# Attention with a soft mixture of experts: another order of steps in the pair loop, another pacing of the weight loads, another tail

## The chip, the cores and the metric

The kernel runs on one core of a Trainium2 chip. The metric is device time in microseconds (us) of one execution. A profiled run also has a span, from its first to its last instruction, some 2 us under that time. A run that is over 1.5% above the fastest of the same kernel counts as slow, and only fast runs are compared.

In the lines of the profile PE is TensorE's matmuls, PEld its weight loads, DVE is VectorE, ACT ScalarE and POOL GpSimd; SBUF and PSUM are the memories on the chip. "Clock" is the share of TensorE's full clock that was granted. The DMA share is the mean busy share of the core's 16 DMA engines; 1.06 is what the fullest long stretches show. In brackets stands how long the engine was idle before, and what ended that; "issue" means that it waited for nothing that the profile shows.

## The reference

Eight batches of eight heads, 576 positions of 64 numbers; 16 "beacon" keys and values stand ahead of each head's own. The result of the attention, as x of shape (4608, 512), goes through a soft mixture of eight experts.

```python
# attention, for each of 64 heads
scores = scale * q @ concat(beacon_k, k).T        # 576 x 592, causal on the last 576
a = exp(scores - max); a /= a.sum(-1)
x = a @ concat(beacon_v, v)
# soft mixture of experts, over all 4608 tokens
logits = x @ phi                                  # 4608 x 32
d = softmax(logits, axis=0)                       # over tokens
slot_input = d.T @ x                              # 32 slots x 512, four for each expert
slot_out[e] = relu(slot_input[e] @ w1[e]) @ w2[e] # w1: 512 x 1024, w2: 1024 x 512
out = softmax(logits, axis=1) @ slot_out
```

The column softmax runs over all tokens, so the experts can't begin before the last head is done, and no output before the last expert.

## The kernel before

Two heads make a pair; 32 pairs run one after the other. For a pair, TensorE turns q and k (`Tq`, `Tk`), makes scores in four steps (`s0` to `s3`) that alternate between two PSUM buffers, ScalarE takes exponentials, GpSimd masks the diagonal blocks, TensorE multiplies with v for the pair before (`a0`, `a1`), and VectorE normalizes. x is turned (`xt`) for the logits (`lg`); once a batch the slot inputs are summed (`dt`, `si`).

The experts' weights are 33.5 MB in HBM. They come in 32 pieces, cast to 16 bits on the way, on GpSimd's DMA queue. q and k come on SyncE's queue, five pairs ahead.

```python
def load_w(i):                       # one piece: 1 MB read, 512 KB written
    ...
    nc.gpsimd.dma_start(out=arena[:, wloc[m]:wloc[m] + WP], in_=src)

wl = 0
for n in range(NP):                  # 32 pairs
    if n < 6:
        head(n)
    else:
        for op in ("s0", "s1", "V", "Tq", "a0", "lg", "s2", "Tk", "s3", "dt", "si", "a1", "xt"):
            step(op, n, b, g)
    ...                              # v loads of later batches, also on GpSimd's queue
    want = n if n < 6 else n - (n - 1) // 4 if n < 24 else 18 + 9 * (n - 23) // 5
    while wl < min(want, NPC):       # pieces asked for by the end of pair n
        load_w(wl)
        wl += 1
while wl < NPC:
    load_w(wl)
    wl += 1
```

After the loop: the last pair's attention, its x turned, logits, slot inputs, then the experts, first layer two steps ahead of the second, and the output.

```python
for p in range(EP + 2):              # EP = 4 steps of two experts
    if p < EP:
        first_layer(p)
    if p == 1:
        col_sums(0, 1)
        slot_factors()
    if 0 < p <= EP:
        turn_hidden(p - 1)
    if p > 1:
        second_layer(p - 2)
```

The softmax here doesn't subtract the row's maximum and nothing guards it: scores larger than these inputs give would overflow.

## Time and profile before

| | before |
|---|---|
| time, median of 4 runs | 197.15 us (195.99 to 200.28) |
| span of the profiled run | 194.7 us |
| first exponential of pair 6, of pair 31 | 37.5 us, 144.7 us |
| last weight piece landed | 163.05 us |
| first output issued | 168.0 us |

Read the table as a chain: loop, tail with experts, output. The output itself, 9.4 MB, takes the 26.7 us from 168.0 to the end. The lines of the profile behind it are in the prediction below.

### The profile page before, as it was taken

What the parts mean: (1) busy time and instruction counts of PE and PEld (TensorE: products, weight loads), DVE (VectorE), ACT (ScalarE), POOL (GpSimd) and SP (SyncE); (2) the same over time, 40 slices, a digit from 0 to 9 for tenths busy, and PEclk for the clock granted to TensorE, in tenths of its full rate; (3) what the DMA queues carried; (4) which work ended last, traced back from release to release, by engine and by line L of the source; (5) the groups of instructions that cost most, each with busy time, mean ns of one, the idle gap of its engine ahead of it and who ended that gap; (6) DMA issues with size and microseconds to landing.
All of it is one profiled execution on the core that took longest, in us unless ns stands there. A gap on an engine that the chain in (4) does not pass through costs nothing. (4 is left out here: it accounts for less than half of the span.)

```text
span 194.7 us, 7324 instructions
## 1 busy us (share of the span) xinstructions
PE 156.7 (81%) x3123; PEld 106.8 (55%) x3123; DVE 138.6 (71%) x286; ACT 128.3 (66%) x175; POOL 112.5 (58%) x293
## 2 busy tenths in 40 slices
PE   6778986779999888968999799988878699887400
PEld 2445765646776665646767566656656544454100
DVE  5537697578989888985799699788657342799700
ACT  2697763748997778775889678877795222578500
POOL 8659893945897597778778687666756100000000
PEclk9955899979999999996999999999999889999955
DMA  6999999999999999999999999999999990399994
GB/s 183 264 240 350 271 242 266 280 261 265 311 261 265 260 276 258 278 255 304 272 282 260 255 293 261 256 254 222 211 213 215 213 186 19 105 380 417 416 428 199
DMA packets 20464, 50.84 MB, mean 261 GB/s; under 512 B 5456, under 2 KB 5456, under 8 KB 19408
## 3 DMA queue, kind: packets, MB, share of 16 engines
q0 software_dynamic: 8048, 21.74, 56.3%
q1 hardware_dynamic: 12240, 28.35, 40.6%
q8 instruction: 24, 0.39, 0.8%
q10 hardware_dynamic: 144, 0.29, 0.5%
q14 instruction: 8, 0.07, 0.1%
HBM read 62.65 MB, written 9.44 MB: 370 GB/s over the span
## 5 line engine op out<-in xcount | busy, mean ns | idle before, releaser
L294 ACT ACTIVATE ex<-sc 128x736 f16<-128x736 f32 (+1 forms) x124 | 101.5, 870 | 27.4 <-PE sc L287 25.4
L296 POOL TENSOR_SCALAR_AFFINE_SELECT ex<-ex 128x256 f16<-128x256 f16 (+1 forms) x155 | 57.3, 399 | 31.4 <-ACT ex L294 31.0
L287 PE MATMUL sc<-qT,kT 64*128 64x336 bf16 (+5 forms) x384 | 44.9, 302 | 4.4 <-ACT ex L294 2.1
L309 PEld LDWEIGHTS <-ex 128*128 128x128 f16 (+1 forms) x930 | 37.5, 108 | 16.9 <-issue 14.8
L309 PE MATMUL av<-vh,ex 128*128 128x65 f16 x840 | 39.6, 200 | 6.3 <-issue 3.4
L270 PE MATMUL tr<-idb,arena 64*64 64x64 bf16 x1152 | 32.0, 201 | 6.6 <-DMA arena<-in_k_dram 2.3
L270 PEld LDWEIGHTS <-arena 64*64 64x64 bf16 x1152 | 25.4, 114 | 20.2 <-issue 13.3
L276 DVE COPY kT<-tr 128x576 bf16<-128x576 bf16 x27 | 20.4, 756 | 9.6 <-PE tr L270 9.6
L320 DVE TENSOR_TENSOR xb<-av,r 128x640 f16<-128x640 f32 x31 | 25.6, 825 | 1.1
L276 DVE COPY qT<-tr 128x576 bf16<-128x576 bf16 x32 | 23.2, 725 | 4.0 <-PE tr L270 3.9
L287 PEld LDWEIGHTS <-kT 64*128 64x128 bf16 (+1 forms) x384 | 15.9, 102 | 14.1 <-issue 6.1
L151 DVE STREAM_TRANSPOSE vh<-vbuf 128x256 f32<-128x256 f32 x32 | 20.4, 657 | 3.3 <-DMA vbuf<-in_beacon_v_dram 1.9
L183 POOL DMA_DIRECT2D arena<-in_moe_w_dram x32 | 17.9, 560 | 0.2
L698 ACT ACTIVATE arena<-fp,rc 128x512 f32<-128x512 f32 (+1 forms) x18 | 11.3, 677 | 7.4 <-PE fp L696 5.9
L127 POOL DMA_DIRECT2D vbuf<-in_v_dram x27 | 15.1, 571 | 0.2 <-DVE xb L320 0.2
L340 DVE COPY xT<-tr 128x592 f16<-128x592 f16 x31 | 13.9, 455 | 1.0 <-PE tr L332 1.0
L332 PE MATMUL tr<-idh,xb 128*128 128x128 f16 (+1 forms) x160 | 14.2, 221 | 0.1
L700 DVE TENSOR_SCALAR arena<-fp,rc 128x512 f32<-128x512 f32 (+1 forms) x19 | 13.1, 732 | 1.2 <-PE fp L696 0.4
L696 PE MATMUL fp<-soh,eLh 128*128 128x512 f16 (+1 forms) x37 | 10.6, 373 | 2.5 <-ACT arena L698 1.7
L319 DVE RECIPROCAL r<-av 128x10 f32<-128x10 f32 x31 | 6.8, 218 | 7.9 <-PE av L309 7.5
L332 PEld LDWEIGHTS <-xb 128*128 128x128 f16 (+1 forms) x160 | 10.4, 103 | 1.1 <-issue 0.9
L696 PEld LDWEIGHTS <-eLh 128*128 128x128 f16 x37 | 3.9, 114 | 5.7 <-issue 4.5
(101 smaller groups left out, 135.6 us busy)
## 6 DMA issues: line engine op xcount, KB each, us to landing
arena<-in_moe_w_dram POOLq DMA_DIRECT2D x32, 512.0 KB, 10.0
arena<-in_q_dram SPq DMA_DIRECT2D x32, 288.0 KB, 14.6
arena<-in_k_dram SPq DMA_DIRECT2D x31, 288.0 KB, 14.9
out_dram<-arena SPq DMA_DIRECT2D x8, 1024.0 KB, 7.2
vbuf<-in_v_dram POOLq DMA_DIRECT2D x30, 128.0 KB, 8.4
arena<-in_v_dram POOLq DMA_DIRECT2D x4, 128.0 KB, 8.4
out_dram<-arena SPq DMA_DIRECT2D x2, 256.0 KB, 3.5
out_dram<-arena SPq DMA_DIRECT2D x1, 512.0 KB, 4.0
```

Of the source, the lines that this page charges most:

```text
L127: nc.gpsimd.dma_start(out=vbuf[b % 2][32 * qd:32 * qd + 32, :], in_=bass.AP(tensor=v.tensor, offset=v.offset + lo, ap=[hs_, cs_, [1, TK * ...
L151: nc.vector.transpose(out=dst[:, e], in_=src.bitcast(FP).rearrange("p (j e) -> p e j", j=TK)[:, e])
L183: nc.gpsimd.dma_start(out=arena[:, wloc[m]:wloc[m] + WP], in_=src)
L270: nc.tensor.transpose(tp[po:po + 64, j, :], hi, idb[po:po + 64, po:po + 64])
L276: nc.vector.tensor_copy(out=dst, in_=src)
L287: nc.tensor.matmul(sc[0:kn, a, col:col + un], kT[n % 3][64 * a:64 * a + 64, P * c:P * c + kn], qT[n % 3][64 * a:64 * a + 64, u0:u0 + un], ...
L294: nc.scalar.activation(e, sc[:, :, 0:w], AF.Exp, scale=scale)
L296: nc.gpsimd.affine_select(out=e[0:m, :, o:o + m], in_=e[0:m, :, o:o + m], compare_op=AL.is_ge, fill=0.0, base=0, pattern=[[0, 2], [1, m]], ...
L309: nc.tensor.matmul(dst[0:m, i * DD:(i + 1) * DD], ex[n][0:kn, o + a * w:o + a * w + m], vchunk(b, 2 * g + a, c, kn), start=(c == 0), stop= ...
L320: nc.vector.tensor_tensor(out=xb[b % 2][:, :, 2 * g:2 * g + 2, :].rearrange("p i a d -> p a i d"), in0=avv[:, :, :, 0:D], in1=r5[:, :, :]. ...
L332: nc.tensor.transpose(tp[:, i, 0:m], xb[b % 2][0:m, i, 2 * g:2 * g + 2, :].rearrange("p h d -> p (h d)"), idh[0:m, 0:m])
L696: nc.tensor.matmul(fp_[:, c], etok(cg, j), soh[:, c], start=True, stop=True)
```

## The change

Its intent: ask for fewer weights while the loop runs, so that q, k and v get the DMA engines, and load the rest behind the loop; place q's turn and x^T so that ScalarE waits less for scores; and take work out of the way between the loop and the experts, with three filler matmuls to keep TensorE's clock up. `warm_tail(3)` makes the three fillers, matmuls whose results nobody uses. At the end of pair 31, 22 instead of 32 pieces are asked for.

```diff
-            for op in ("s0", "s1", "V", "Tq", "a0", "lg", "s2", "Tk", "s3", "dt", "si", "a1", "xt"):
+            for op in ("s0", "Tq", "s1", "V", "a0", "xt", "s2", "Tk", "s3", "lg", "a1", "dt", "si"):
                 step(op, n, b, g)
...
-        want = n if n < 6 else n - (n - 1) // 4 if n < 24 else 18 + 9 * (n - 23) // 5
+        want = n // 2 if n < 24 else 12 + 5 * (n - 23) // 4
...
     for rows in ((4,), (3, 2, 1), (0,)):
-        if rows == (0,):
-            spread_rows(0, nc.vector)
         for a in range(2):
             attend_blocks(...)
...
+    fold_si(0)
     logits(L, lp, [0, 1, 2])
-    fold_si(0)
+    xt_piece(NP - 1)
     fold_si(1)
-    xt_piece(NP - 1)
     logits(L, lp, [3])
     logit_exp(L, lp)
-    spread_rows(1, nc.scalar)
+    spread_rows(0, nc.scalar)
...
+    warm_tail(3)
     dt_piece(L)
...
-    spread_ends(0, 4, nc.scalar, av[:, 1, 128:128 + 4 * UL])
...
         if p < EP:
             first_layer(p)
+        if p == 0:
+            spread_ends(0, 4, nc.scalar, av[:, 1, 128:128 + 4 * UL])
+            spread_rows(1, nc.scalar)
```

More of the change, by code (lines that the diff above doesn't have):

```diff
@@ L602, with warm_tail @@
     lp = scs[1][:, 0, 0:ZW]
+    fold_si(0)
     logits(L, lp, [0, 1, 2])
-    fold_si(0)
+    xt_piece(NP - 1)
     fold_si(1)
-    xt_piece(NP - 1)
     logits(L, lp, [3])
     logit_exp(L, lp)
-    spread_rows(1, nc.scalar)
+    spread_rows(0, nc.scalar)
+    def warm_tail(k):
+        for _ in range(k):
+            nc.tensor.matmul(scs[0][:, 1, :], idh[:, :], xTs[L % 2][:, 0:512],
+                             start=True, stop=True)
+    warm_tail(3)
     dt_piece(L)
```

## The prediction

> **What bounds the kernel now.** I read four views in this order: the slices of the page with the two transfer queues, the stretches, the timeline of ScalarE in the attention loop, and the timeline of the tail. First the slices: DMA busy share, GB/s, and the share of 16 engines that each queue's packets took.
>
> ```profile
> DMA  6999999999999999999999999999999990399994
> GB/s 183 264 240 350 271 242 266 280 261 265 311 261 265 260 276 258 278 255 304 272 282 260 255 293 261 256 254 222 211 213 215 213 186 19 105 380 417 416 428 199
> ...
> q0 software_dynamic: 8048, 21.74, 56.3%
> q1 hardware_dynamic: 12240, 28.35, 40.6%
> ```
>
> The reader is to see that the 16 DMA engines are full from slice 2 to slice 33, that is up to about 161 us, then idle for about 7 us, then full again with the output. Queue 0 carries the MoE weights and v, which GpSimd issues; queue 1 carries q, k and the output. The stretches (us from:to, length, busy time of PE, PEld, DVE, ACT, POOL, clock, DMA share, GB/s) say it in numbers:
>
> ```profile
> 48.00:130.00 82.00, 73.55 (x1714) 53.24 (x1712) 70.10 (x135) 65.07 (x83) 62.78 (x167) 0.98 1.06 271
> 138.00:155.00 17.00, 12.99 (x250) 9.60 (x249) 9.06 (x21) 10.48 (x16) 9.46 (x26) 0.97 1.06 213
> ...
> 161.00:166.00 5.00, 5.00 (x88) 2.10 (x80) 1.07 (x3) 0.73 (x2) 0.00 (x0) 1.00 0.05 11
> ```
>
> A share of 1.06 is the most the engines show. From 138 us on only weights move: 213 GB/s written, so a 512 KB piece costs 524288/213e3 = **2.46 us**. What one pair of heads asks, in engine time: queue 1 took 40.6% of 194.7 = 79.0 us; the output is 9.44 MB at 400 GB/s, 23 us; the rest, 56 us, is q and k, or 1.75 us for each of 32 pairs. Queue 0 took 109.6 us; 32 weight pieces are 32 x 2.46 x 1.06 = 83.4; the rest, 26.2, is v, or 0.82 a pair. The old pacing asks for 3 pieces in 4 pairs, 0.75 x 2.61 = 1.95. The sum is 4.52, and over 1.06 it is **4.27 us a pair**. ScalarE's timeline has the first exponential of pair 6 at 37.46 and of pair 30 at 141.05: 24 pairs in 103.6 us, 4.32 each. So the loop runs at the rate of the DMA engines. What it could do without them is seen where data had come early: pairs 20 and 21 start at 99.74 and 103.19, pair 22 at 106.76, so 3.45 to 3.57 us.
>
> ```profile
> 37.46 1.40 ACT L294 ACTIVATE ex<-sc 128x736 f16<-128x736 f32 x2
> ...
> 99.74 4.86 ACT L294 ACTIVATE ex<-sc 128x736 f16<-128x736 f32 x6 [0.59 <-PE sc L287]
> ...
> 141.05 1.41 ACT L294 ACTIVATE ex<-sc 128x736 f16<-128x736 f32 x2 [0.80 <-PE sc L287]
> ```
>
> Then the tail: the last two weight issues, the end of the second expert layer, its scaling, the first outputs.
>
> ```profile
> 148.81 1.08 POOL L183 DMA_DIRECT2D arena<-in_moe_w_dram  x2
> ...
> 164.16 1.91 PE L665 MATMUL av<-arena,hbuf 128*32 128x512 f16 x32
> 166.00 0.11 PEld L696 LDWEIGHTS <-eLh 128*128 128x128 f16 x1 [0.42 <-issue]
> 166.13 0.88 DVE L684 TENSOR_SCALAR soh<-av,rd 128x256 f16<-128x256 f32 x2 [1.43 <-PE av L665]
> ...
> 168.00 2.35 SPq L704 DMA_DIRECT2D out_dram<-arena  x3
> ```
>
> The last piece is issued at 149.35 and, with the longest landing of that line (13.7 us), is there at **163.05**. The second layer ends at 166.07, so today the experts' arithmetic ends last (TensorE is busy all of 161 to 166), but only 3 us behind the weights. From the first output issue at 168.0 to the end at 194.7 is the drain of the output, 26.7 us.
>
> **What the Trainium skill says.** "DMA: Bandwidth & Descriptors", section "Issuing engines are not separate DMA queues", says that transfers started by different engines run on the same 16 DMA engines and interleave. The trace agrees: the two queues' shares sum to 0.97 of the whole span, and the share stays at 1.06 whatever the mix. So a weight piece held back makes room for q and k, but takes its 2.46 us later. "TensorE: Matmul & The Clock Gate", Part 1, says that TensorE's clock falls to half after an idle window of about 3.4 us and returns after about as long a busy one. The trace agrees in size: the clock record has 0.5 from 153.9 to 157.3, just after the thin stretch between attention and experts. "Perfetto Trace Analysis", section "What "DMA-bound" means", names the engines themselves as one kind of DMA bound; that is this case, not slow issue.
>
> **The change, part by part.**
>
> (a) Pacing. floor(n/2) pieces up to pair 23, then 12 + floor(5(n-23)/4): 11 instead of 18 pieces after pair 23, 22 instead of 32 after pair 31, so ten are issued after the loop. A pair now asks 1.75 + 0.82 + 0.5 x 2.61 = 3.88, over 1.06, **3.66 us**. That is about the engines' own pace: over the 82 us stretch, some 19.6 pairs, TensorE was busy 3.75 us a pair and VectorE 3.58, including the per-batch work. I take 3.75 us on average, and 2 us gained before pair 6, where fewer pieces are asked. First exponential of pair 31: 35.5 + 25 x 3.75 = 129.3, against 144.7 now. So the loop should end some **15 us earlier**.
>
> (b) But the weights go the other way. The last issues start 4.1 us after that exponential (148.81 - 144.72): 133.4. Then 12 pieces are outstanding (10, and the 2 of the last pair): 12 x 2.46 = 29.5, and 2 us for the last to be counted as landed (traffic ends near 161, the landing is 163.05). That gives **164.9**. There is a floor too: the bytes before the output are the same, and the engines were full to 161, so the last piece can't land before about 163 however the loop runs. Each us in which the engines find nothing asked moves it later. From pair 24 on only 1.25 x 2.46 = 3.1 us are asked in a pair of 3.75, so some idle time is sure.
>
> (c) Order of steps. No instruction is added in the loop. q's turn between the score steps puts 0.4 us of TensorE work where it waited 0.2 us for a score buffer, so perhaps 0.1 us a pair; x^T in the middle and the logits after the last scores are neutral in sum. It lies inside a loop that no longer sets the end.
>
> (d) Tail. One spread with its 0.68 us VectorE copy leaves the attention of the last pair; a second spread and the ends' spread go behind the first expert layer; three filler matmuls (about 0.3 us each) are added. All of it now lies in front of a wait for weights: the experts begin near 142, the last piece comes at 165. It costs and gains nothing.
>
> (e) After the last landing four matmuls remain (about 0.5 us), then 1.9 us as now from the end of the layer to the first output: 167.4, against 168.0. But TensorE has by then waited in steps of 2.46 us with little work, so the output starts on a half clock: in 170 to 182 TensorE is busy 10.04 of 12 us at full clock, so I add 1 us. Sum: 167.4 + 1 + 26.7 = 195.1 us of span, against 194.7; in the metric, times 197.34/194.7, **197.7**; I write 197.5.
>
> **The rivals.** First: the loop gain comes through. For it: 15 us at the loop's end, and the experts' 10.7 us could overlap loading. Against: the full DMA engines; even at the 163 us floor the first output comes at 165.4 and the gain is 2.6 us, 1.3%. Over 2% needs q and k packets to get cheaper in the new mix. Time then: 194 to 195, a little less with cheaper packets. Second: the loop stays slow for other reasons (the "issue" waits of TensorE, VectorE at 3.6 us a pair), 3.9 us a pair. The DMA engines then idle in the loop, and the last piece lands near 169: about 201 to 202. Third: GpSimd's ten issues (5.5 us) delay the memsets behind them; but those are wanted only before the output, so nothing.
>
> **Range and chances.** The middle estimate is 0.1% over now; 0.15 us a pair is 4 us at the end on the slow side, while the fast side is cut off by the floor. The three times of before spread by 2%. Range 193.0 to 201.5; faster 0.13, within 2% 0.70, slower 0.17.
>
> **What would show it.** Right: pair 31's exponential near 129, DMA share still 1.0 in most of the loop, weights alone from about 120 to 163, the second layer's last matmuls waiting for a weight DMA, the first output between 166 and 170. Wrong: the last weight landed well before 162 (then bytes became cheaper), or DMA slices under 0.8 in the loop (then idle, and slower), or a tail waiting for something other than weights.

## The result, and the profile after

The changed kernel takes **210.61 us** (210.33 to 210.90, 4 runs), against 197.15 us. The ratio is 1.070, 95% interval 1.065 to 1.076. A ratio here is the mean time of one kernel's fast runs over that of the other's fast runs of the same rounds, so it isn't quite the ratio of the medians quoted beside it. The prediction said 197.5 us, 193.0 to 201.5, and was wrong.

The page of the changed kernel, DMA busy share, rate and the two queues:

```profile
DMA  6999999999998899799899999999999999189994
GB/s 189 265 266 340 290 285 259 280 290 301 244 249 268 196 244 283 192 207 261 217 236 246 241 182 168 175 176 163 179 213 213 214 214 184 41 320 411 416 426 206
...
q0 software_dynamic: 8048, 21.74, 56.2%
q1 hardware_dynamic: 12240, 28.35, 37.9%
```

The same bytes move, but some slices of the loop stand at 7 or 8, slices 24 to 29 carry only 163 to 182 GB/s, and the full stream of weights (213) runs on to about 178 us. Next, the stretches of both kernels: loop from pair 6 to pair 31, then to the last weight landing, to the first output, to the end (from:to, length, busy PE, PEld, DVE, ACT, POOL, clock, DMA share, GB/s). Before:

```profile
37.46:144.72 107.26, 95.14 (x2179) 68.50 (x2179) 88.41 (x170) 83.96 (x109) 78.53 (x208) 0.97 1.06 263
144.72:163.05 18.33, 15.31 (x243) 9.52 (x246) 8.53 (x24) 7.39 (x13) 5.30 (x14) 0.91 0.91 183
163.05:168.00 4.95, 4.24 (x61) 2.05 (x53) 2.20 (x6) 0.94 (x3) 0.00 (x0) 1.00 0.01 2
168.00:194.70 26.70, 12.59 (x94) 6.98 (x91) 14.97 (x29) 12.20 (x22) 0.00 (x0) 0.81 0.87 354
```

After:

```profile
36.34:140.63 104.29, 94.31 (x2183) 67.96 (x2182) 88.73 (x170) 82.09 (x108) 75.61 (x202) 0.98 0.98 233
140.63:178.59 37.96, 21.37 (x290) 11.39 (x290) 9.18 (x25) 8.24 (x14) 10.04 (x23) 0.81 0.99 191
178.59:181.28 2.69, 2.04 (x9) 0.76 (x9) 1.44 (x4) 0.47 (x1) 0.00 (x0) 0.50 0.00 0
181.28:208.70 27.42, 13.98 (x96) 7.58 (x94) 15.15 (x29) 12.74 (x22) 0.00 (x0) 0.81 0.85 345
```

The loop got only 3.0 us shorter and began 1.1 us earlier, so pair 31 came 4.1 us sooner. The stretch from there to the last weight grew from 18.3 to 38.0 us, by 19.6. After the landing 2.3 us were gained, because the experts' arithmetic no longer lags behind; the output took 0.7 us more. The sum, -4.1 + 19.6 - 2.3 + 0.7, is the 14 us of the spans. TensorE's timeline of the changed kernel shows what the end hangs on:

```profile
173.73 0.40 PE L669 MATMUL av<-arena,hbuf 128*32 128x512 f16 x4 [1.49 <-DMA arena<-in_moe_w_dram]
176.15 0.40 PE L669 MATMUL av<-arena,hbuf 128*32 128x512 f16 x4 [2.02 <-DMA arena<-in_moe_w_dram]
178.64 0.62 PE L669 MATMUL av<-arena,hbuf 128*32 128x512 f16 x4 [2.08 <-DMA arena<-in_moe_w_dram]
```

Each last piece comes some 2.46 us after the one before it, and TensorE does four matmuls and waits again. GpSimd's timeline shows the issues of those pieces:

```profile
144.65 3.73 POOL L183 DMA_DIRECT2D arena<-in_moe_w_dram  x7
...
149.15 0.54 POOL L183 DMA_DIRECT2D arena<-in_moe_w_dram  x1 [0.77 <-DMA arena<-in_moe_w_dram]
...
159.22 0.53 POOL L183 DMA_DIRECT2D arena<-in_moe_w_dram  x1 [1.95 <-DMA arena<-in_moe_w_dram]
```

Twelve pieces were still to be issued at 144.65. After seven, GpSimd stands until an earlier piece lands. The packed trace shows why it stops there: GpSimd's DMAs use eight semaphores in turn (109 to 116), and each issue waits until the transfer before on its own semaphore has landed, so this program has at most eight under way. With nothing under way, eight are issued in 4.3 us and the ninth waits (late_old). Behind it stand its zero fills, and behind those TensorE, for long:

```profile
PE av L367 <- POOL eLh L617: 10.1, 1, 10.1
```

That is the longest single wait of TensorE in the changed kernel. Whether it costs anything is one of the questions below.

### The profile page after: what moved, and what is told of

Same layout as the page of the kernel before. It is cut to its first block, busy times and chain, and to the rows that moved or that the text cites.

```text
span 208.7 us, 7327 instructions
## 1 busy us (share of the span) xinstructions
PE 160.8 (77%) x3126; PEld 107.4 (51%) x3126; DVE 138.2 (66%) x285; ACT 127.6 (61%) x176; POOL 112.9 (54%) x293
## 5 line engine op out<-in xcount | busy, mean ns | idle before, releaser
L287 PE MATMUL sc<-qT,kT 64*128 64x336 bf16 (+5 forms) x384 | 46.5, 298 | 3.6 <-ACT ex L294 2.1
L309 PEld LDWEIGHTS <-ex 128*128 128x128 f16 (+1 forms) x930 | 36.9, 107 | 20.6 <-issue 12.8
L309 PE MATMUL av<-vh,ex 128*128 128x65 f16 x840 | 38.8, 199 | 9.1 <-DVE xb L320 5.2
L270 PEld LDWEIGHTS <-arena 64*64 64x64 bf16 x1152 | 24.7, 113 | 12.0 <-issue 7.2
L276 DVE COPY qT<-tr 128x576 bf16<-128x576 bf16 x32 | 23.9, 746 | 4.0 <-PE tr L270 3.9
L287 PEld LDWEIGHTS <-kT 64*128 64x128 bf16 (+1 forms) x384 | 16.5, 100 | 14.4 <-issue 6.2
L340 DVE COPY xT<-tr 128x592 f16<-128x592 f16 x31 | 13.3, 435 | 5.3 <-PE tr L332 5.3
L332 PE MATMUL tr<-idh,xb 128*128 128x128 f16 (+1 forms) x160 | 13.7, 216 | 0.6 <-issue 0.5
L703 PE MATMUL fp<-soh,eLh 128*128 128x512 f16 (+1 forms) x37 | 12.0, 425 | 2.1 <-ACT arena L705 1.5
L367 PEld LDWEIGHTS <-rept 128*128 128x128 f16 x41 | 3.3, 111 | 12.6 <-issue 11.6
```

What stands on the lines that cost most here:

```text
L270: nc.tensor.transpose(tp[po:po + 64, j, :], hi, idb[po:po + 64, po:po + 64])
L276: nc.vector.tensor_copy(out=dst, in_=src)
L287: nc.tensor.matmul(sc[0:kn, a, col:col + un], kT[n % 3][64 * a:64 * a + 64, P * c:P * c + kn], qT[n % 3][64 * a:64 * a + 64, u0:u0 + un], ...
L309: nc.tensor.matmul(dst[0:m, i * DD:(i + 1) * DD], ex[n][0:kn, o + a * w:o + a * w + m], vchunk(b, 2 * g + a, c, kn), start=(c == 0), stop= ...
L332: nc.tensor.transpose(tp[:, i, 0:m], xb[b % 2][0:m, i, 2 * g:2 * g + 2, :].rearrange("p h d -> p (h d)"), idh[0:m, 0:m])
L340: nc.vector.tensor_copy(out=xTs[b % 2][:, g * U:(g + 1) * U], in_=src)
```

## The experiments

All kernels below were correct. "Pieces late" is the number of weight pieces issued after pair 31's first exponential; the loop is pair 6 to pair 31, 25 pairs. All but the two time columns are from one profile each.

| kernel | time us (median) | ratio to before | us a pair | pair 31 | pieces late | last landing | first output |
|---|---|---|---|---|---|---|---|
| before | 197.15 | 1 | 4.29 | 144.7 | 4 | 163.1 | 168.0 |
| changed | 210.61 | 1.070 | 4.17 | 140.6 | 13 | 178.6 | 181.3 |
| pace_tail | 210.92 | 1.068 | 4.23 | 142.2 | 12 | 179.0 | 181.7 |
| pace_only | 207.57 | 1.056 | 4.05 | 137.8 | 13 | 175.1 | 177.8 |
| order_only | 197.54 | 1.002 | 4.33 | 146.1 | 4 | 162.6 | 169.7 |
| order_tail | 194.84 | 0.988 | 4.24 | 144.8 | 4 | 162.0 | 165.7 |
| tail_only | 194.79 | 0.988 | 4.28 | 143.9 | 4 | 163.1 | 165.4 |
| pace_mid | 201.76 | 1.023 | 4.12 | 140.1 | 9 | 169.0 | 171.7 |
| pace_full | 206.66 | none given | 4.62 | 156.2 | 2 | 165.3 | 177.0 |
| pe_fill | 201.59 | 1.017 | 4.41 | 147.6 | 4 | 163.0 | 171.7 |
| memset_dve | 209.78 | 1.062 | (profile of a slow run) | | | | |
| late_old | 250.70 (one run) | | 3.87 | 132.7 | 32 | 218.9 | 221.5 |
| late_new | 253.62 (one run) | | 3.94 | 135.6 | 32 | 221.8 | 224.5 |
| late_pool | 253.41 (one run) | | 3.90 | 134.4 | 32 | 222.0 | 224.7 |

### Which part of the change costs

My first theory blamed the order. In the changed loop TensorE waits for VectorE's normalization and for GpSimd's masks where it did not before, because only 1 us of other work lies between one attention half and the next. Four kernels take the three parts apart.

pace_tail, the changed kernel with the old order:

```diff
-            for op in ("s0", "Tq", "s1", "V", "a0", "xt", "s2", "Tk", "s3", "lg", "a1", "dt", "si"):
+            for op in ("s0", "s1", "V", "Tq", "a0", "lg", "s2", "Tk", "s3", "dt", "si", "a1", "xt"):
```

> The changed kernel with the old order of steps (new pacing and tail kept). Theory O (the new order holds the loop at 4.17 us a pair although the data lie ready, and the late weights turn each us of the loop into a us at the end): the old order runs at about 3.8 us a pair, the last ten weight issues start some 9 us earlier, 200 to 203 us. Rival I (4.17 us a pair is the loop's own pace in either order, so before was never held by its loads): 208 to 212 us, as the changed kernel.

pace_only, the kernel before with `want = n // 2 if n < 24 else 12 + 5 * (n - 23) // 4`:

> The kernel before with the new pacing alone. Theory O: loop at about 3.8 us a pair, 200 to 203 us, as with the tail. Rival I: 208 to 212 us. If this is over 3 us from the run that has the new tail as well, the tail matters.

order_only, the kernel before with the new order:

> The kernel before with the new order alone. Theory O: the loop was held at 4.3 us a pair by the transfers anyway, so an order whose own pace is 4.17 hides behind them: 197 to 200 us. Rival I: same as before within 1%. Both would be wrong if it is over 202 us.

order_tail, the changed kernel with the old `want`:

> The changed kernel with the old pacing of weights (new order and tail kept). If the pacing is what puts the end late, as both theories say, the last weight lands near 163 to 166 us and the time is 196 to 200 us. A third theory (the tail's spreads behind the memsets of GpSimd cost by themselves) would leave it at 204 us or more.

Measured: pace_tail 210.92 us (ratio 1.068, interval 1.047 to 1.089), pace_only 207.57 (1.056, 1.047 to 1.065), order_only 197.54 (1.002, 0.998 to 1.007), order_tail 194.84 (0.988, 0.984 to 0.992). The theory of the order falls: with the old order back, the loop still takes 4.23 us a pair, and the order alone moves nothing that can be measured. (Theory O's 3.8 us a pair came in neither kernel, rival I's 4.17 only in pace_tail; order_tail came out under the expected 196 to 200.) The pacing alone makes the kernel 5.6% slower, and without it the rest of the change is 1.2% faster than before. So the pacing is the cause of the loss, in either order and with either tail. That pace_only came out 3.4 us under pace_tail doesn't show that the tail costs: the intervals overlap, and in pace_tail's profile the loop alone, before the tail, was 4.6 us longer.

```profile
36.34:142.19 105.85, 94.85 (x2181) 68.34 (x2180) 88.68 (x171) 84.02 (x109) 75.72 (x204) 0.98 0.98 233
```

```profile
36.55:137.75 101.20, 92.68 (x2179) 67.25 (x2179) 88.20 (x171) 83.86 (x108) 75.19 (x202) 1.00 1.00 240
```

These are loops of the same steps (pace_tail first). They differ in TensorE's clock, 0.98 and 1.00, and in its waits for "issue", 5.5 and 2.4 us; both are taken up below. Loops of single profiles can thus differ by almost 0.2 us a pair without any difference in their steps.

### The tail alone, and half of the pacing

tail_only is the kernel before with the new tail; pace_mid is the kernel before with

```diff
-        want = n if n < 6 else n - (n - 1) // 4 if n < 24 else 18 + 9 * (n - 23) // 5
+        want = 5 * n // 8 if n < 24 else 14 + 3 * (n - 23) // 2
```

> The kernel before with the new tail alone. The run with new order and new tail was 1.2% faster and the new order alone even, so the tail should be what gained: 1 to 1.5% faster than before, first output about 2 us nearer to the end of the loop. If it is even with before, the gain of the pair comes from the two together.

> The kernel before with a pacing between the two: 26 of 32 weight pieces asked by the last pair, 6 left for after the loop (before: 2, changed: 10). Theory W (each piece held past the loop costs its 2.46 us at the end, once the last landing lies behind the experts' arithmetic): last piece lands about 166 to 168 us, first output 169 to 171, 198 to 201 us. Rival (the slowness comes from the change of regime, as GpSimd's blocked queue): 196 to 198 us, as before.

tail_only: 194.79 us, ratio 0.988 (0.980 to 0.996), as expected. In this kernel the experts catch up with the weights. Its stretch from pair 31 to the last landing, and TensorE at the end:

```profile
143.89:163.06 19.17, 17.70 (x290) 10.41 (x290) 8.71 (x24) 8.03 (x14) 5.32 (x14) 1.00 0.88 177
```

```profile
163.10 0.40 PE L669 MATMUL av<-arena,hbuf 128*32 128x512 f16 x4 [0.50 <-DMA arena<-in_moe_w_dram]
164.09 1.31 PE L703 MATMUL fp<-soh,eLh 128*128 128x256 f16 x5 [0.59 <-DVE soh L691]
```

The clock is 1.00 here, against 0.91 in the same stretch before; the fillers and the denser work were meant for that. The last four matmuls wait only 0.5 us for the last piece, and the first output goes out 2.4 us after it, against 4.95 before. Little is left to gain between weights and output. Fillers and moved spreads were not tried apart.

pace_mid: 201.76 us, 1.023 (1.014 to 1.031). The landing, 169.0, lies just over the expected 166 to 168, and so do the first output and the time. With it there is a scale: from pair 31 to the last landing it is 18.3 us with 4 pieces late, 28.9 with 9, 38.0 with 13, and 86.1 with 32 (late_old). That is 2.1, 2.3 and 2.5 us a piece, near the 2.46 us of a piece at 213 GB/s. **Every piece that is held past the loop costs its transfer time at the end**, once the arithmetic has nothing left to hide it.

### What the loop would do without weights

> The kernel before with no weight piece in the loop at all (all 32 after it). Only its loop matters. Theory T (TensorE's own instruction stream paces the loop in every version): 3.9 to 4.1 us a pair although a third of the bytes is gone. Theory D (the transfers pace it, as the prediction had it): 3.5 to 3.7 us a pair. The time will be near 240 us, as 32 pieces of 2.46 us follow the loop.

> The changed kernel with no weight piece in the loop (all 32 after it): the new order's own pace. The old order's own pace was measured at 3.87 us a pair. If the order is neutral, 3.8 to 3.95 us a pair; if its shorter way from one attention half to the next costs (TensorE waited 5.2 us for VectorE's normalization and 8.7 us for the masks), 4.05 or more.

late_old is the kernel before and late_new the changed one, each with `want = 0`. Their loops (late_old first):

```profile
35.88:132.72 96.84, 91.77 (x2179) 66.99 (x2179) 87.86 (x171) 83.92 (x109) 66.41 (x185) 1.00 0.61 155
```

```profile
37.06:135.62 98.56, 91.93 (x2183) 67.04 (x2182) 88.30 (x170) 81.73 (x109) 66.40 (x186) 1.00 0.60 153
```

With no weights in the loop at all and the DMA engines at 0.6, a pair takes 3.87 us in the old order and 3.94 in the new (one run each, on two chips, so the 0.07 between them is not shown to be the order's). TensorE is busy for 91.8 of 96.8 us. So **the loop's own pace is 3.9 us a pair**, set by TensorE's stream with few gaps, and the pacing could have gained 0.4 us a pair at most, by these profiles. Theory T is right here (3.87 lies just under its 3.9 to 4.1), and the 3.75 of the prediction was too small.

### Is it GpSimd's time, or the traffic

Theory G is that GpSimd's time for the issues slows the loop. late_pool puts, in late_old, a fill of a scratch area in the place of each issue:

```diff
-            load_w(wl)
+            nc.gpsimd.memset(arena[:, 0:600], 0.0)
             wl += 1
+    wl = 0
     while wl < NPC:
```

> As the run with all weights after the loop (old order), but GpSimd fills a scratch area for about 0.55 us wherever the kernel before issues a weight piece: GpSimd's time without the traffic. Theory D (the traffic itself slows the loop): pace stays 3.85 to 3.95 us. Theory G (GpSimd's issue time holds up the masks): 4.2 to 4.3 us, as before.

```profile
36.93:134.37 97.44, 91.86 (x2179) 67.01 (x2179) 87.91 (x171) 83.80 (x108) 78.93 (x209) 1.00 0.60 155
```

The loop takes 3.90 us a pair, with GpSimd busy 78.9 us, as in the kernel before (78.5). Theory G falls, by one run: what slows the loop by 0.2 to 0.4 us a pair comes with the transfers, not with GpSimd's time. The view of waits of TensorE's matmuls shows where. In late_old's loop the longest rows are these (us in total, times, longest):

```profile
PE av L309 <- POOL ex L296: 1.0, 1, 1.0
PE tr L410 <- DVE qT L276: 0.4, 1, 0.4
PE tr L270 <- DVE qT L276: 0.4, 1, 0.4
```

and in the loop of the kernel before:

```profile
PE av L309 <- issue: 3.9, 7, 1.0
PE tr L270 <- DVE qT L276: 2.1, 2, 1.4
PE tr L270 <- DMA arena<-in_k_dram: 1.4, 1, 1.4
PE tr L346 <- issue: 0.9, 1, 0.9
```

Waits for "issue", in which nothing that the profile shows is waited for, are absent without weights and come to about 5 us with them; the changed kernel has about 3. They are instruction fetch, by two signs. Queue 8, of kind "instruction", carries 24 packets of 16 KB; TensorE has 6246 instructions, so a packet is one for about 256 of them, one in 6 us. Each such gap over 0.25 us in the loops of before (9), changed (5) and pace_only (2) ends 1.3 to 1.7 us after the end of one of these packets. And all 51 gaps of that kind, in nine kernels with weights in the loop, stand at the same place of TensorE's stream: if its instructions are counted in order of start from 0, the number of the matmul leaves 193 when divided by 256. pace_full has none, although its engines are as full (1.04); there TensorE stands for k and q instead, as shown below. No run changed the fetch alone.

### Does TensorE pace the loop before

pe_fill adds six matmuls without use to each pair of the kernel before:

```diff
                 step(op, n, b, g)
+                if op == "a0":
+                    for _ in range(6):
+                        nc.tensor.matmul(av[:, 0, 384:512], idh[:, :], idh[:, :],
+                                         start=True, stop=True)
```

> The kernel before with six small matmuls without use (128x128, into a free part of a PSUM bank) after the first attention half of each pair from 6 on, some 0.35 to 0.4 us of TensorE a pair. Theory T: TensorE paces the loop, which gets longer by all of it, 9 to 10 us over 26 pairs, 204 to 207 us. Theory D: they disappear in the wait for transfers, the loop grows by under 3 us, 197 to 200 us.

```profile
37.30:147.55 110.25, 101.45 (x2329) 73.83 (x2329) 89.50 (x171) 84.08 (x108) 79.38 (x209) 1.00 1.05 259
```

Neither theory is right. TensorE's busy time in the loop grew by 6.3 us (95.1 to 101.5), the loop by 3.0 us (107.3 to 110.3), so 3.3 us of its idle time went. But the fillers are more than these 6.3 us, for the clocks differ. The page's row of the clock, of before and of pe_fill:

```profile
PEclk9955899979999999996999999999999889999955
```

```profile
PEclk9996997999999999999999999999999969999955
```

In the loop of before the clock stood at half twice, for 3.4 us from 41.2 and from 89.0; in that of pe_fill never. Against late_old, whose loop is at full clock too (busy 91.8), the fillers are 9.7 us of work. Of these 3.3 went into waits that were there, 3.4 were made up by the clock, and 3.0 lengthened the loop. The same account fits the other kernels: take half of the time at half clock from TensorE's busy time in the loop, and all of them but pe_fill come to 91.7 to 92.9 us (pace_full 90.0). So of the 10.4 us that the loop of before is longer than late_old's, 3.4 come from the half clock and 7.0 are more idle time, about 5 of it the fetch waits. What lowered the clock is not shown; the loops of pace_only and pace_mid stayed at 1.00 without fillers.

The time, 201.59 us (1.017, 1.008 to 1.027), grew by about as much as the first output moved (168.0 to 171.7). The loop before seems to lie near both limits: its arithmetic needs 3.87 us, measured without the weights, and its transfers about 4.27 by the prediction's sum, which no run measured alone. pace_full goes the other way, the new tail with one piece a pair:

```diff
+        want = n + 1
```

> The kernel before with the new tail and one piece a pair from the start, so that nothing is left for after the loop. If the sum of bytes before the output is the floor of the last landing, it still lands at 161 to 164 us and no earlier; the loop itself gets slower, pair 31 at 146 to 150 us, and the experts end 20 us after that: 195 to 199 us, not faster than the new tail with the old pacing (194.8). Rival: earlier weights come earlier, last landing under 158 us.

206.66 us; half of its runs fell in the slow state, so no interval is given, but its fast runs (204.6 and 205.3) lie over the fast runs of before in those rounds (195.4 and 198.1). Now TensorE does wait for q and k:

```profile
PE tr L270 <- DMA arena<-in_k_dram: 8.6, 8, 1.9
PE tr L270 <- DMA arena<-in_q_dram: 4.0, 6, 1.2
```

The loop takes 4.62 us a pair and pair 31 comes at 156.2, later than the expected 146 to 150; the time was expected at 195 to 199. The last landing is at 165.3, so pieces asked for earlier did not make it earlier; but the experts, 20.9 us behind pair 31, now set the end. Between the two failures lies the old pacing: few pieces left at the end, and a loop that isn't starved.

### The longest wait of the changed kernel

memset_dve moves GpSimd's three zero fills and one copy behind the loop to VectorE (`nc.gpsimd.memset(eLz...)` to `nc.vector.memset(eLz...)`, and the copy to `foldr` likewise).

> The changed kernel with the three zero fills and the copy that wait behind GpSimd's blocked weight issues moved to VectorE. In the changed kernel TensorE stood 10.1 us before them. If the last weight landing sets the end, this is worth nothing: 210 to 211 us, ratio to before 1.06 to 1.075, TensorE then stands before the weights instead. If the standing in the tail counts, it gains 3 us or more.

209.78 us, ratio 1.062 (1.038 to 1.087): no gain that could be told from noise. Its profiled run was slow, so of that profile I use only what TensorE waited for in its place:

```profile
PE sc L655 <- DMA arena<-in_moe_w_dram: 11.2, 3, 5.5
```

The 10.1 us before the fills became 11.2 us before the weights. The long wait lay ahead of a later release on the same path, and so its removal gained nothing that shows.

## Why the prediction was wrong, point by point

**The bound of the loop.** The prediction found 4.27 us of transfers a pair, saw 4.32 and concluded that the loop runs at the rate of the DMA engines. The two numbers agree, but the conclusion was only half true: with the weights gone the loop still needs 3.87, and with more work on TensorE it grew (by 3.0 us for 9.7 us of fillers). There was a sign in the trace of before: pairs 24 to 31 start at 116.24 and 144.72, which is 4.07 us a pair, while the k of pair 31 had landed at 135.87, over 2 us before pair 29 turned it, and TensorE waited for no data there. That stretch was not read. The Trainium skill warns of this reading: "Perfetto Trace Analysis", section "Identifying the Most-Contended Engine", says that with 16 DMA engines occupancy misleads. Here the share was 1.06 in a loop that added TensorE work still lengthened. (The prediction also read the half clock from 153.9 as that of an idle window. Its length, 3.4 us, agrees, but TensorE wasn't idle: it was busy for 2.15 of the 3.4 us before, and for 2.00 and 1.87 of the 3.4 us before the two half-clock stretches in the loop.)

**Part (a), the step that failed: "I take 3.75 us on average".** It is TensorE's busy time divided by the pairs, and it left out the gaps. (The busy time itself is a little short: 48 to 130 us holds 19.3 pairs by ScalarE's timeline, not 19.6, which gives 3.81.) The loop took 104.3 us instead of 25 x 3.75 = 93.8. Of these 10.5 us, the loop's own pace in the new order explains 4.8 (98.6 us in late_new), and what comes with the traffic of the weights the other 5.7: TensorE's idle time grew by about 3.4 us, about as much as its waits for "issue" (3.2), and its busy time by 2.4 at a clock of 0.98 instead of 1.00, with one stretch of 3.4 us at half clock. The sizes are of single profiles; pace_tail and pace_only show that such a split can shift by 4.6 us. The prediction took the larger of two nearly equal limits, 3.66 and 3.75, as the pace; measured was more than either.

**Part (b), the link from the loop to the end.** Its mechanism was right, and it named the landing as the thing to watch: 164.9. Measured is 178.6. Of the 13.7 us, 0.8 come from the start of pair 6, 10.5 from (a), and 2.4 from the last twelve pieces, which took 33.9 us instead of 31.5, since pieces already under way stood in front: the first landed 6.9 us after its issue, the other eleven at 2.46 us each. The "floor" of 163 us was right as a floor (no run landed before 162.0), but the prediction put the changed kernel within 2 us of it.

**Part (c), the order.** Right: neutral, 1.002 (0.998 to 1.007). The expected 0.1 us a pair did not come; without weights the new order was 0.07 slower, which is within what single profiles differ by.

**Part (d), the tail.** "It costs and gains nothing" fits the changed kernel, where the weights hide it: the first output comes 2.7 us after the last landing, with the old tail (pace_only) as with the new. It was worth 1.2% by itself, which the prediction did not look for.

**Part (e)** was right to 0.1 us: from the last landing to the end 30.1 us were estimated (0.5 + 1.9 + 1 + 26.7) and 30.1 measured (2.7 + 27.4), with the clock at 0.50 up to the first output.

**The rivals and the range.** The second rival is what happened: 3.9 us a pair, landing near 169, 201 to 202 us. It got 17% for anything over 2% slower, and even it was not pessimistic enough, at 4.17. Each 0.1 us of a pair is 2.5 us at the end; with a pace that uncertain, a range of 8.5 us was too narrow. Its sign of being wrong, a DMA slice under 0.8 in the loop, showed in one slice. The third rival (GpSimd's issues) was rightly put at nothing.

## What to carry to other kernels

Where transfers and arithmetic need nearly the same time, the pace of a loop can lie above both, as here (4.17, against 3.66 and 3.94); find each by taking the other away, as was done here for the transfers only, and don't read it from busy time divided by count. Loads that can be spread over a long loop should be, as long as the loop isn't starved: what is left for behind the loop costs its full transfer time, and here eight or nine more late pieces cost far more than the 4 us that the loop gave back. Of the runs here the best is the old pacing with the new tail, at 194.8 us in either order.

## What the Trainium skill lacked or had wrong

- "Runtime: NRT & Kernel Launch", section "Instruction fetch mechanics", says that instructions are fetched in 16 KiB blocks of 256 over a DMA queue, and that the cost of a block boundary is mostly hidden. The blocks are there (24 packets of 16 KB for TensorE), but the cost isn't always hidden: with weights in the loop TensorE stood at such boundaries, 256 instructions apart, for about 5 us in the loop before, up to 1 us at a time (2.2 in pace_tail), and not at all in the loops without weights. Full DMA engines alone don't bring it about: pace_full, at a share of 1.04, has no such gap. That the transfers delay the fetch is read from the traces, not shown by a run of its own.
